# Lightning attention followed by a gated MLP on one core: attention rewritten in units of two heads, with row- and column-tiled matmuls in a fixed order on TensorE

## Chip, cores and metric

The kernel runs on one core of one Trainium2 chip. The metric is device time in microseconds (us) of the whole program. Every time quoted is a median of several executions, with the lowest and highest where they matter. An execution counts as fast or slow: slow is one that lies over 1.5% above the fastest of the same kernel. Medians are of all executions, ratios of fast ones alone.

The engines are TensorE (PE in the profile; PEld is its weight load), VectorE (DVE), ScalarE (ACT), GpSimd (POOL) and SyncE (SP). A line number such as L215 is a line of the kernel that was profiled; experiments that add lines shift the numbers, so each fence is to be read by the names of its tiles.

## The reference

Linear attention with a decay per head, for 4 batches, 8 heads, 768 positions and head size 64, and then an MLP whose gate mixes positions. Cut to what matters:

```python
def _attn_ref(q, k, v, lam):                     # blocks of 64 positions
    for b in range(nb):
        intra = einsum('bhic,bhjc->bhij', qb, kb) * Dmask    # lam ** (i - j) for i >= j
        intra = einsum('bhij,bhjd->bhid', intra, vb)
        inter = einsum('bhid,bhde->bhie', qb * lam_pow, kv_state)
        out[:, :, sl] = intra + inter
        kb_dec = kb * rev_pow                                # lam ** (block - 1 - j)
        kv_state = lam_block * kv_state + einsum('bhsd,bhse->bhde', kb_dec, vb)

def _moe_ref(x, w_in, w_spatial, b_spatial, w_out):          # x: 4 x 768 x 512
    h = maximum(x @ w_in, 0)                                 # 1024 columns
    u, v = h[..., :512], h[..., 512:]
    v_n = (v - mean(v)) / sqrt(var(v) + 1e-6)
    v_s = einsum('ts,bsd->btd', w_spatial, v_n) + b_spatial
    return (u * v_s) @ w_out
```

Both kernels use blocks of 128 positions rather than 64, which is the same function. In both, the 16 units of work are (batch, pair of heads), and the MLP of a batch can start once its four units are done.

## The kernel before

For each unit, stage A loads and transposes q and k; stage B goes through the six blocks one at a time. Per block it issues one score matmul for both heads (q is held as a block-diagonal with zeros in half of it), two matmuls for the state, two for the product with v and two for the old state. One piece of work of the MLP goes between blocks. These are the parts that the change touches:

```python
loglam = const.tile([P, H], FP32)
nc.scalar.activation(out=loglam, in_=lam_bc, func=AF.Ln)
# ... (four more Ln, one per pair of heads, from loads of lam of their own)
nc.scalar.activation(out=ldech, in_=loglam, func=AF.Exp, scale=i127mp[:, 0:1])
# ... (more Exp; ScalarE ends up changing between Ln and Exp)

# stage B of unit u: attention of one pair of heads
def issue_akv(m):
    pam = psum.tile([P, 384], FP32, tag="bank", name=f"pam_{u}_{m}")
    nc.tensor.matmul(out=pam[:, 0:256], lhsT=kT[:, m * P:(m + 1) * P],      # full array
                     rhs=qT_bd[:, :, m * P:(m + 1) * P], start=True, stop=True)
    for hh in range(2):
        nc.tensor.matmul(out=pam[hh * 64:(hh + 1) * 64, 256:320],           # 64 columns
                         lhsT=kdec[:, m, hh, :], rhs=v_sb[:, m, hh, :],
                         start=True, stop=True)

for m in range(NBLK):
    # ... VectorE: mask of the scores (256 elements), new state
    if m + 1 < NBLK:
        issue_akv(m + 1)
    for hh in range(2):
        nc.tensor.matmul(out=pout[orows, ocols], lhsT=v_sb[:, m, hh, :], rhs=a_sb[:, hh, :], ...)
        if m > 0:
            nc.tensor.matmul(out=pout[orows, ocols], lhsT=sold,
                             rhs=qT_bd[:, hh, m * P:(m + 1) * P], ...)
    # ...
    yield

# driver
for u in range(NU):
    gB, gA = ...                                  # stage B of u, stage A of u + 3
    for step, _ in enumerate(gB):
        # ... next(gA)
        if fi < len(fillers):
            fillers[fi](); fi += 1                # transposes of w_spatial
        elif moe_pend:
            moe_pend.pop(0)()                     # one piece of the MLP
```

## Time and profile before

| | before |
|---|---|
| time | 218.57 us, median of 3 (218.17 to 220.46) |
| span of the profiled execution | 221.2 us |
| TensorE busy | 188.9 us (85%) |
| VectorE, ScalarE busy | 128.0, 115.4 us |
| changes of tiling on TensorE | 278 |

A page is read from the top: the busy shares say which engine could be the bound; the 40 slices say when; the chain that ended last says what each part of the time waited for. A busy TensorE need not be streaming columns. For that I take the trace of its instructions and walk from the start of each matmul to the start of the next. From each interval I take the columns at the clock then granted (0.056 us for 128 columns, 0.107 at half clock; these are measured). If two neighbours have different tilings (rows by columns of the array in use), up to 0.13 us of the rest is put down to the change of tiling. What then remains is waiting. Columns that run at half clock are counted at the full rate, with the loss put in a row of its own. This account is used throughout. It adds up to the span. The trace of before lacks 9 of its 1412 matmul records, all of 512 columns, so some 2 us of its columns appear as waits. The columns of one and the same kernel come out 2 to 3 us apart from run to run, so differences below that are not read from it.

### The profile page before, as it was taken

How to read it: one execution, taken by the hardware profiler on the slowest of the kernel's cores; microseconds unless marked ns; L12 is line 12 of the kernel's file. 1: busy time of each engine (PE TensorE's matmuls, PEld its weight loads, DVE VectorE, ACT ScalarE, POOL GpSimd, SP SyncE). 2: the span in 40 equal slices, each digit the busy share in tenths (PEclk: the TensorE clock that was granted, in tenths of full speed). 3: DMA queues.
4: the chain of work that ended last, by engine and by line, in shares of the span. 5: the costliest groups of instructions: out<-in, count | busy, mean ns of one | idle time of the engine just before them, and what ended most of it. 6: DMA issues, size and time to landing. Idle time of an engine off the chain costs nothing.

```text
span 221.2 us, 3795 instructions
## 1 busy us (share of the span) xinstructions
PE 188.9 (85%) x1403; PEld 102.2 (46%) x1412; DVE 128.0 (58%) x355; ACT 115.4 (52%) x217; POOL 83.1 (38%) x110
## 2 busy tenths in 40 slices
PE   0204988899899989999997999999999999998992
PEld 0202644556555556644444455554444565454640
DVE  5106676446879783865789717784698544181420
ACT  7997431666957982116265733023435901679032
POOL 8999144973799771553522200202000000000000
PEclk9999999999999999999999569999999999999998
DMA  4999999993999998959995130506700000700025
GB/s 26 114 130 153 205 186 162 135 126 24 101 108 120 119 66 56 74 70 141 225 66 36 12 27 0 36 3 98 225 3 0 0 3 0 285 0 0 3 90 195
DMA packets 81505, 18.92 MB, mean 86 GB/s; under 512 B 76496, under 2 KB 77904, under 8 KB 81488
## 3 DMA queue, kind: packets, MB, share of 16 engines
q0 software_dynamic: 77248, 12.39, 75.4%
q1 hardware_dynamic: 4240, 6.30, 8.0%
q8 instruction: 11, 0.18, 0.4%
q14 instruction: 6, 0.05, 0.1%
HBM read 24.78 MB, written 6.29 MB: 140 GB/s over the span
## 4 chain that ended last, share of the span: by engine, by line
PE 59%; DMA 14%; POOL 12%; DVE 6%; ACT 4%; issue 3%; ACTq 0%; POOLq 0%
PE pvs L336 14%; PE pu L322 8%; DMA wsp_raw<-in_moe_w_spatial_dram 8%; PE po L354 7%; PE pv L295 7%; PE pam L233 5%; PE pam L236 4%; PE pout L262 4%; POOL q_sb L179 3%; POOL k_sb L181 3%; PE pvs L339 2%; DMA out_dram<-o_sb 2%; DMA k_sb<-in_k_dram 2%; DVE qbd L207 2%; ACT vn_sb L313 2%
## 5 line engine op out<-in xcount | busy, mean ns | idle before, releaser
L250 DVE TENSOR_TENSOR a<-pam,qlkm 128x256 bf16<-128x256 f32 x96 | 39.6, 419 | 15.1 <-PE pam L236 14.5
L185 POOL DMA_DIRECT2D v_sb<-in_v_dram x28 | 23.3, 853 | 51.7 <-PE pout L266 37.9
L233 PE MATMUL pam<-qbd,kT 128*128 128x256 bf16 x96 | 30.8, 321 | 9.7 <-ACT kT L213 9.5
L336 PE MATMUL pvs<-wt_sb,vn_sb 128*128 128x384 bf16 x192 | 37.0, 326 | 1.0 <-ACT vn_sb L313 0.7
L254 DVE SCALAR_TENSOR_TENSOR sst<-sst,l,pam 128x64 bf16<-128x64 bf16 x96 | 26.1, 272 | 14.6 <-PE pout L266 11.7
L358 ACT ACTIVATE o_sb<-po 128x512 f32<-128x512 f32 x24 | 14.3, 597 | 34.2 <-PE po L354 28.8
L342 DVE TENSOR_TENSOR gatedT<-pvs,uT 128x384 bf16<-128x384 f32 x32 | 17.8, 558 | 24.7 <-PE pvs L339 24.6
L262 PE MATMUL pout<-a,v_sb 128*64 128x128 bf16 x192 | 27.1, 256 | 5.1 <-DVE a L250 5.0
L181 POOL DMA_DIRECT2D k_sb<-in_k_dram x28 | 24.6, 887 | 10.4 <-ACT kdec L189 5.2
L322 PE MATMUL pu<-xT,win_sb 128*128 128x384 bf16 x128 | 26.9, 356 | 1.4 <-DVE qbd L207 1.4
L179 POOL DMA_DIRECT2D q_sb<-in_q_dram x28 | 24.4, 879 | 7.1 <-PE pam L236 4.6
L336 PEld LDWEIGHTS <-vn_sb 128*128 128x128 bf16 x192 | 18.3, 98 | 14.0 <-ACT vn_sb L313 1.6
L189 ACT ACTIVATE kdec<-k_sb,ldech 128x384 bf16<-128x384 bf16 x32 | 18.2, 606 | 12.7 <-PE pam L236 10.9
L236 PE MATMUL pam<-v_sb,kdec 128*64 128x64 bf16 x192 | 23.9, 233 | 0.0
L295 PE MATMUL pv<-win_sb,xT 128*128 128x512 bf16 x93 | 23.0, 380 | 0.5 <-DVE qbd L207 0.3
L354 PE MATMUL po<-wout_sb,gatedT 128*128 128x512 bf16 x90 | 22.5, 380 | 0.7 <-DVE qbd L207 0.4
L298 ACT ACTIVATE vh<-pv 128x512 bf16<-128x512 f32 x24 | 14.3, 597 | 13.3 <-PE pv L295 13.0
L299 DVE BATCH_NORM_STATS2 st<-vh 128x6 f32<-128x512 bf16 x24 | 16.6, 690 | 7.6 <-ACT vh L298 7.4
L266 PE MATMUL pout<-qbd,sst 128*64 128x128 bf16 x160 | 20.8, 249 | 0.0
L207 DVE TENSOR_TENSOR qbd<-pqt,lq 64x768 bf16<-64x768 bf16 x32 | 17.7, 553 | 5.4 <-PE pqt L199 4.9
L262 PEld LDWEIGHTS <-v_sb 128*64 128x64 bf16 x192 | 14.7, 121 | 13.1 <-issue 9.8
L236 PEld LDWEIGHTS <-kdec 128*64 128x64 bf16 x192 | 12.2, 116 | 18.2 <-issue 14.5
(63 smaller groups left out, 224.1 us busy)
## 6 DMA issues: line engine op xcount, KB each, us to landing
out_dram<-o_sb SPq DMA_DIRECT2D x24, 256.0 KB, 2.0
q_sb<-in_q_dram POOLq DMA_DIRECT2D x32, 96.0 KB, 3.9
k_sb<-in_k_dram POOLq DMA_DIRECT2D x32, 96.0 KB, 3.8
v_sb<-in_v_dram POOLq DMA_DIRECT2D x32, 96.0 KB, 3.8
wsp_raw<-in_moe_w_spatial_dram POOLq DMA_DIRECT2D x1, 1152.0 KB, 17.2
win_sb<-in_moe_w_in_dram POOLq DMA_DIRECT2D x1, 1024.0 KB, 8.7
wout_sb<-in_moe_w_out_dram POOLq DMA_DIRECT2D x1, 512.0 KB, 10.5
bspbc_sb<-in_moe_b_spatial_dram POOLq DMA_DIRECT2D x1, 192.0 KB, 11.1
```

Source lines behind the costliest of these rows:

```text
L179: nc.gpsimd.dma_start(out=q_sb[:, :, hh, :], in_=q[b, h].rearrange("(m p) d -> p m d", p=P))
L181: nc.gpsimd.dma_start(out=k_sb[:, :, hh, :], in_=k[b, h].rearrange("(m p) d -> p m d", p=P))
L185: nc.gpsimd.dma_start(out=v_sb[:, :, hh, :], in_=v[b, h].rearrange("(m p) d -> p m d", p=P))
L233: nc.tensor.matmul(out=pam[:, 0:256], lhsT=kT[:, m * P:(m + 1) * P], rhs=qT_bd[:, :, m * P:(m + 1) * P], start=True, stop=True)
L236: nc.tensor.matmul(out=pam[hh * 64:(hh + 1) * 64, 256:320], lhsT=kdec[:, m, hh, :], rhs=v_sb[:, m, hh, :], start=True, stop=True)
L250: nc.vector.tensor_tensor(out=a_sb, in0=pam[:, 0:256].rearrange("p (h c) -> p h c", c=P), in1=qlkm_g[g], op=ALU.mult)
L254: nc.vector.scalar_tensor_tensor(out=snew, in0=sold, scalar=lam128_g[g][:, 0:1], in1=pam[:, 256:320], op0=ALU.mult, op1=ALU.add)
L262: nc.tensor.matmul(out=pout[orows, ocols], lhsT=v_sb[:, m, hh, :], rhs=a_sb[:, hh, :], start=True, stop=(m == 0))
L295: nc.tensor.matmul(out=pv, lhsT=xT[gg][:, nt * P:(nt + 1) * P], rhs=win_sb[:, gg, DH:DFF], start=(gg == 0), stop=(gg == NCH - 1))
L322: nc.tensor.matmul(out=pu, lhsT=win_sb[:, gg, ft * P:(ft + 1) * P], rhs=xT[gg][:, b * S + th * THW: b * S + (th + 1) * THW], start=(gg == ...
L336: nc.tensor.matmul(out=pvs, lhsT=vn_sb[:, nt, dc * P:(dc + 1) * P], rhs=wt_sb[:, st, th * THW:(th + 1) * THW], start=(st == 0), stop=False)
L354: nc.tensor.matmul(out=po, lhsT=gatedT[:, ft, nt * P:(nt + 1) * P], rhs=wout_sb[:, ft, :], start=(ft == 0), stop=(ft == NCH - 1))
```

## The change

The intent is to spend less of TensorE's time between matmuls. The work of a unit is put in blocks of equal shape: all transposes, then six scores, ten state matmuls, ten and twelve output matmuls. Scores use two row tiles (64 rows each, one head in each, so that no half is zeros). The decays move into k, into q and into a single mask, which needs fewer operations on VectorE. A whole batch of q, k and v comes in three transfers (the first batch in parts). The order of TensorE's instructions is fixed by hand, with four pieces of the MLP at a time. The core of the diff:

```diff
-            nc.tensor.matmul(out=pam[:, 0:256], lhsT=kT[:, m * P:(m + 1) * P],
-                             rhs=qT_bd[:, :, m * P:(m + 1) * P], start=True, stop=True)
-            for hh in range(2):
-                nc.tensor.matmul(out=pam[hh * 64:(hh + 1) * 64, 256:320],
-                                 lhsT=kdec[:, m, hh, :], rhs=v_sb[:, m, hh, :],
-                                 start=True, stop=True)
+        pam = ps_a.tile([P, 2, 4, P], FP32, tag="pam", name=f"pam_{u}_{i}")
+        for c in range(3):
+            for hh in range(2):
+                t = 3 * i + c
+                nc.tensor.matmul(out=pam[:, hh, c, :],
+                                 lhsT=kT[hh * D:(hh + 1) * D, t * P:(t + 1) * P],
+                                 rhs=qblk(u, hh, t), start=True, stop=True)
 ...
+        for c in range(1, NBLK):                 # outputs from the states: 64 x 64 tiles
+            for hh in range(2):
+                rows = slice(hh * D, (hh + 1) * D)
+                nc.tensor.matmul(out=po[c // 3][rows, c % 3, :], lhsT=s_sb[rows, c - 1, :],
+                                 rhs=qblk(u, hh, c), start=c in (1, 3), stop=False,
+                                 skip_group_check=True)
+        for c in range(NBLK):                    # outputs from the masked scores: 128 x 64
+            for hh in range(2):
+                rows = slice(hh * D, (hh + 1) * D)
+                nc.tensor.matmul(out=po[c // 3][rows, c % 3, :], lhsT=v_in[b][:, 2 * g + hh, c, :],
+                                 rhs=a_sb[:, hh, c, :], start=False, stop=c in (2, 5),
+                                 skip_group_check=True)
 ...
-            nc.scalar.activation(out=vn_sb[:, nt, :], in_=vh_sb[:, st, :],
-                                 func=AF.Identity,
-                                 bias=nbias[:, st:st + 1], scale=rstd[:, st:st + 1])
+                    nc.vector.tensor_scalar(out=vn[:, s, :], in0=vh[:, s, :],
+                                            scalar1=mv[:, s, 0:1], scalar2=rstd[:, s:s + 1],
+                                            op0=ALU.subtract, op1=ALU.mult)
 ...
+    with tc.manual_schedule(engines={PE}):
+        # ... units 0 and 1 are begun
+        for u in range(NU):
+            b, g = divmod(u, NG)
+            if u + 2 < NU:
+                gate = kdec_unit(u + 2)
+                if u + 2 == NG - 1:
+                    load_batch(1, gate)          # k by SyncE after the gate; q, v by GpSimd
+            if g == 2 and b + 2 < B:
+                load_batch(b + 2, gate)
+            if u + 1 < NU:
+                scores_unit(u + 1, 0)
+            out_unit(u)
+            # ... at g == 3 the pieces of batch b join the list
+            fill(4)
+            if u + 1 < NU:
+                scores_unit(u + 1, 1)
+                kv_unit(u + 1)
+            if u + 2 < NU:
+                trans_unit(u + 2)
+            fill(4 if u % 2 else 3)
```

Cuts are marked "...".

## The prediction

> **What bounds the kernel now.** I read the page first (busy shares, the 40 slices, the chain), then the timeline of a dense stretch, of the start and of the cold part, then the groups by form.
>
> ```profile
> PE 188.9 (85%) x1403; PEld 102.2 (46%) x1412; DVE 128.0 (58%) x355; ACT 115.4 (52%) x217; POOL 83.1 (38%) x110
> ...
> PE   0204988899899989999997999999999999998992
> ...
> PEclk9999999999999999999999569999999999999998
> ...
> PE 59%; DMA 14%; POOL 12%; DVE 6%; ACT 4%; issue 3%; ACTq 0%; POOLq 0%
> ```
>
> TensorE (PE) is busy in nearly every slice from 20 us on and is 59% of the chain that ended last; the other 26% of DMA and POOL lie in the first 72 us. So there are two parts: a start that waits, then a PE that sets the pace. But busy is not streaming. The timeline of a warm, dense stretch:
>
> ```profile
> 86.25 1.14 PE L336 MATMUL pvs<-wt_sb,vn_sb 128*128 128x384 bf16 x6
> ...
> 87.39 0.50 PE L199 MATMUL pqt<-ident,q_sb 128*128 128x128 bf16 x6
> 87.73 0.27 PE L233 MATMUL pam<-qbd,kT 128*128 128x256 bf16 x1
> 87.93 0.22 PE L236 MATMUL pam<-v_sb,kdec 128*64 128x64 bf16 x2
> 87.98 0.23 PE L262 MATMUL pout<-a,v_sb 128*64 128x128 bf16 x2
> 88.04 0.22 PE L266 MATMUL pout<-qbd,sst 128*64 128x128 bf16 x2
> ...
> 88.60 0.27 PE L233 MATMUL pam<-qbd,kT 128*128 128x256 bf16 x1
> 88.81 0.22 PE L236 MATMUL pam<-v_sb,kdec 128*64 128x64 bf16 x2
> 88.96 0.28 PE L233 MATMUL pam<-qbd,kT 128*128 128x256 bf16 x1
> ```
>
> Six 384-column matmuls span 1.14 us and one lasts 0.326 (group mean), so (1.14-0.326)/5 = 0.162 us each; six 128-column transposes give (0.50-0.219)/5 = 0.056. Two 64-row-output matmuls of a pair start together (x2 in 0.22), so a pair costs one: 87.98 to 88.04 is 0.056 for a 128-column pair, 87.93 to 87.98 is 0.05 for a 64-column pair. But from a full-array matmul to a column-tiled pair it takes 88.60 to 88.81 = 0.21 us, where 256 columns stream in 0.107; and back 88.81 to 88.96 = 0.15 for 64 columns. Each change of tiling costs about 0.1 us. Walking the whole PE trace with these stream times I get 278 changes at 0.11 us = 31 us, and 28 us of gaps beyond streaming and changes, 10 of them before 20 us. The rest, some 158 us, is streaming (136 us if all of it were warm, below) and the end.
>
> The start:
>
> ```profile
> 8.16 0.69 PE L199 MATMUL pqt<-ident,q_sb 128*128 128x128 bf16 x5 [8.16 <-DMA q_sb<-in_q_dram]
> ...
> 19.61 0.40 PE L233 MATMUL pam<-qbd,kT 128*128 128x256 bf16 x1 [9.52 <-ACT kT L213]
> ...
> 26.02 0.85 PE L199 MATMUL pqt<-ident,q_sb 128*128 128x128 bf16 x6
> ```
>
> Scores begin only at 19.6 us, because ScalarE first does nine table loads of 1.28 us (rows of that name in the groups by form), most of them swaps between Ln and Exp, and then the decay tables. And six transposes take 0.85 us at 26 us against 0.50 at 87: PE runs at half rate (0.107 us per 128 columns) until about 56 us, and again from 121 to 131, where PEclk shows 5 and 6. The chain names what feeds the middle of the start:
>
> ```profile
> 18.65 17.17 DMA wsp_raw<-in_moe_w_spatial_dram
> 35.86 0.49 issue
> 36.35 5.13 DMA k_sb<-in_k_dram
> ```
>
> The weights (2.9 MB as bf16, 5.8 MB read as f32) take until about 36 us, some 330 GB/s of reads; the attention inputs behind them wait.
>
> **What the Trainium skill says.** "TensorEngine Tiling (Array Packing)", Key Properties: changing the tiling mode, not just the tile, drains the engine. The trace agrees: about 0.1 us each. The same page, Gotcha 1 (PSUM Pressure): different row tiles cannot access one PSUM bank at once. No row tile is in this trace; it bears on a rival below. "TensorE: Matmul & The Clock Gate", Part 1: the clock is half when idle and full after sustained activity; the 0.107 against 0.056 agrees. "VectorE: DVE Perf Modes", the perf-mode tier table: a tensor_scalar on bf16 in SBUF can run at four elements a cycle; no row of before is of that sort at size, so I use it only for an estimate.
>
> **The change part by part.** MLP matmuls are the same in number and shape: 224 of 384 columns (pvs with bias) and 128 (pu) at 0.162, 192 of 512 at 0.216 (pv, po) = 36.3+20.7+41.5 = 98.5 us of streaming.
>
> Attention, streaming when warm. Before: 192 transposes x 0.056 = 10.8, 96 scores of 256 columns (half of them zeros) x 0.107 = 10.3, 96 kv pairs x 0.05 = 4.8, 96+80 output pairs x 0.056 = 9.9; 36 wsp transposes 2.0; 37.8 in all. After: transposes of 64 columns in 192 pairs, 10.8; scores 96 row-tiled pairs of 128 columns, 5.4 if the pair runs together; kv 80 pairs, 4.0; outputs 80+96 pairs, 9.9; wsp 2.0; 32.1 in all. So streaming falls only from 136 to 131 us.
>
> Tiling changes: in the instruction order of PE I count 278 before and 104 after (scores, kv, transposes and outputs come in blocks per unit, MLP pieces four at a time). At 0.1 us: 31 to about 10.5 us, a gain of 20 us. This is the largest term.
>
> ScalarE: 7 of the 9 opening table loads go (one for Ln and one for Exp stay), so scores can begin near 11 us rather than 19.6. vn moves to VectorE (17.3 us off; 24 operations there at an estimated 0.25 us = 6), the transposed k is always copied on ScalarE (16 x 0.81 = 12.9 against 6.5), as is every xT (32 x 0.49 = 15.6 against 7.7), wt 6 x 0.81. Sum some 102 us against 115.
>
> VectorE: mask 32 x (0.42-0.267+0.8) = 0.95 for 768 elements (the 256-element row is 0.419, about 0.267 of it elements) = 30.5 against 39.6; states 16 x 0.22 + 64 x 0.272 = 21 against 26; q 16 x 0.56 = 9 against 17.7; no xT or kT copies (13 off); bn and gate unchanged at 38.7; vn 6; setup 3. About 108 against 128. Neither engine becomes the bound: per unit with its MLP pieces PE needs about 9.4 us, VectorE 6.6, ScalarE 5.8.
>
> Loads: q packs two rows (3,072 packets a batch, not 6,144), k goes as f32 by the SP queue. A batch is 4.7 MB read, in three transfers, and unit 4's transposes need the whole q of batch 1, which stands behind the weights. Fixed PE order puts those transposes before the output of unit 3 and so before any MLP of batch 0. Landing estimate: batch 0 4.7 + weights 5.8 + k and q of batch 1 3.1 = 13.6 MB at 330 GB/s = 41 us, plus 2 of latency: 43 to 45 us. Before that, units 0 to 3 have no filler; start 11.5, about 3 of prologue and three rounds of some 5.2 us (mask, mask, states, q on VectorE 3.8, plus waits) end near 30. So PE idles from about 30 to 44.
>
> Path: 44 us; then the PE work left: 131 - 8 (attention of the first units) = 123 streaming, 82 changes x 0.105 = 8.6; a cold first window 2; waits for PSUM in the MLP pieces. For these, before in its warm middle (60 to 180 us) has 9.6 us in 120, 8%; two banks with pu at 0.65 of PE against 0.48 plus latency on ScalarE stay tight; 8% of 131 = 10. End after the last matmul: evacuation 0.6, output transfer 2.0, closing, 4 in all as before. 44+123+8.6+2+10+4 = 191.6. The tail's vn wait of before (about 4 us at 199 to 204) is gone, since pieces of u lie in between. I take 189.
>
> **Rivals.** (1) The pairs do not run together, for the output pairs from the states put two row tiles in one bank: +4.5 us (80 x 0.056), and for scores +5.4: about 199. For: the skill's gotcha. Against: the two halves write different partitions, and scores use two banks. (2) The transfers are faster or in another order and q of batch 1 lands by 36: about 181. For: slice 5 moved 205 GB/s of bf16, over 330 read. Against: 128-byte packets in before never passed 135. (3) ScalarE or VectorE in their given order hold PE in each unit, as two banks and strict order leave no slack: 20 us of waits rather than 10, 200. For: the margin of 0.65 over 0.48 plus latency. Against: in the list of waits of before it is those engines that wait for PE (o_sb 28.8 us, gatedT 24.6), and PE's own waits on them in the MLP are under 2 us each. (4) Another half-clock spell like that of 121 to 131: +5. (5) The waits are nearly gone because the pieces are spread by hand: 181.
>
> **Range and chances.** Rivals move it by 8 to 10 us either way and can add: 189, 8 in 10 from 175 to 203. To be within 2% (214 to 223) at least three of the adverse ones must come together. Faster 0.96, same 0.03, slower 0.01.
>
> **What would show it.** Right: a PE gap near 30 to 44 us ended by the q load of batch 1; changes of tiling near 104 with about 0.1 us each; pairs of scores within 10 ns of each other; PE in 95% of the slices after 45; VectorE near 108 and ScalarE near 102 busy. Wrong: pairs 0.05 us apart (rival 1); no gap at 30 (rival 2); waits of PE on ScalarE or VectorE above 15 us after 45 (rival 3); PEclk below 9 late (rival 4). If changes between row and column tiles cost 0.2 rather than 0.1, +8.

## The result, and the profile after

| | before | after |
|---|---|---|
| time | 218.37 us, median of 4 (217.67 to 220.46) | 198.5 us, median of 4 (198.18 to 198.84) |
| span of the profiled execution | 221.2 us | 196.7 us |
| ratio | | 0.9065, 95% interval 0.9004 to 0.9127 |

A ratio here is the mean time of one kernel's fast runs over the mean of the other's fast runs of the same rounds, so it is not quite the ratio of the medians.

The page of the changed kernel, from busy shares to the shares of the chain:

```profile
PE 153.4 (78%) x1668; PEld 89.3 (45%) x1668; DVE 104.5 (53%) x252; ACT 99.3 (50%) x181; POOL 23.2 (12%) x28
...
PE   0341766103779599999999699999999999999992
...
PEclk9999985555589999999999999999999999999998
DMA  5999999999999939931697000043000004400025
...
PE 59%; DMA 26%; ACT 4%; DVE 4%; POOL 4%; issue 1%; POOLq 0%; ACTq 0%
```

Against the rows of before: TensorE is now nearly idle in slices 8 and 9 and most of 10 (the gap lasts from 35 to 47 us), the DMA share of the chain has risen from 14% to 26%, and the row of the clock shows half from 28 to 56 us. From 59 us on TensorE is busy in nine tenths of each slice or more, but for two slices at 64 and 108 us and the last.

The timeline of TensorE around the gap (start, length, engine, line, tiles, count, and in brackets the idle time before and what ended it):

```profile
34.61 0.48 PE L228 MATMUL pkv<-v_in,kdec 128*64 128x64 bf16 x10
47.21 0.85 PE L187 MATMUL pq<-ident,q_in 128*64 128x128 bf16 x12 [12.12 <-DMA q_in<-in_q_dram]
...
52.44 5.24 PE L285 MATMUL pv<-win_sb,xT 128*128 128x512 bf16 x16
...
59.20 0.35 PE L228 MATMUL pkv<-v_in,kdec 128*64 128x64 bf16 x10 [1.24 <-DMA v_in<-in_v_dram]
```

The transposes of unit 4, the first of batch 1, wait 12.1 us for the whole q of their batch. The first piece of the MLP stands behind them and starts at 52.4 us. The length of 0.85 us for twelve transposes (they run in pairs) shows the half clock.

The timeline of TensorE in a warm stretch, in which a unit's scores and outputs stand between pieces of the MLP:

```profile
101.30 0.34 PE L215 MATMUL pam<-qT,kT 64*128 64x128 bf16 x6
101.57 0.47 PE L247 MATMUL pat<-qT,s 64*64 64x128 bf16 x10
101.97 0.53 PE L253 MATMUL pat<-a,v_in 128*64 128x128 bf16 x12
102.42 1.90 PE L285 MATMUL pv<-win_sb,xT 128*128 128x512 bf16 x8
```

28 attention matmuls take 102.42 - 101.30 = 1.12 us. Six scores in three pairs are 3 x 0.056 = 0.17 of the 0.27 us to the next group, ten state outputs in five pairs 0.28 of 0.40, twelve score outputs in six pairs 0.34 of 0.45. What is left over is 0.10, 0.12 and 0.11 us: one change of tiling each.

The waits of TensorE (us in total, times, longest):

```profile
PE pq L187 <- DMA q_in<-in_q_dram: 21.3, 3, 12.1
PE pam L215 <- ACT kT L198: 8.7, 4, 4.9
...
PE pwt L333 <- ACT wt_sb L335: 2.3, 2, 2.1
PE pkv L228 <- DMA v_in<-in_v_dram: 1.2, 1, 1.2
```

The larger ones lie before 60 us, but for the 2.1 us of the w_spatial transposes (pwt), which wait for their own copies at 65 us. And the groups by line, for the two operations whose cost came out above the estimate:

```profile
L257 ACT ACTIVATE xT<-pat 128x384 bf16<-128x384 f32 x32 | 16.7, 593 | 24.8 <-PE pat L253 24.8
...
L294 DVE TENSOR_SCALAR vn<-vh,mv,rstd 128x512 bf16<-128x512 bf16 x24 | 8.1, 408 | 0.1
```

The account of TensorE's time, by the walk described above:

| us | before | after | difference |
|---|---|---|---|
| until the first matmul | 8.2 | 8.3 | +0.1 |
| columns, at the full rate | 130.9 | 127.0 | -3.9 |
| lost to the half clock | 16.0 | 8.3 | -7.7 |
| changes of tiling (278, 104) | 30.9 | 10.7 | -20.2 |
| waits | 27.7 | 35.8 | +8.1 |
| gaps of at most 0.01 us between matmuls | 2.9 | 2.5 | -0.4 |
| after the start of the last matmul | 4.6 | 4.0 | -0.6 |
| span | 221.2 | 196.7 | -24.5 |

The largest term is the changes of tiling; the new wait for q of batch 1 eats a part of it. One caution belongs to this table: the profiled execution of before is a long one. In all runs the time is some 2 us above the span, so 221.2 us of span is a time of about 223 us (an estimate), where the median is 218.4. The medians differ by 19.9 us and not by 24.5, so about 4.6 us of the last column belong to that execution and not to the change. It ran at half clock from 121 to 131 us, which cost about 4 us in the walk. No trace of a faster execution of before was kept, so how much of the -7.7 us in the row of the half clock comes from the change is not shown. The number of changes of tiling is the same in every execution. The experiments ask three things: is a change of tiling really the cause of the 20 us, what sets the start, and what can be had from it.

### The profile page after: what moved, and what is told of

It reads as the page before. It is cut to its first block, busy times and chain, and to the rows that moved or that the text cites. A ratio compares the mean times of both kernels' runs of the same rounds, so it can differ in the third digit from the quotient of the medians.

```text
span 196.7 us, 3964 instructions
## 1 busy us (share of the span) xinstructions
PE 153.4 (78%) x1668; PEld 89.3 (45%) x1668; DVE 104.5 (53%) x252; ACT 99.3 (50%) x181; POOL 23.2 (12%) x28
## 4 chain that ended last, share of the span: by engine, by line
PE 59%; DMA 26%; ACT 4%; DVE 4%; POOL 4%; issue 1%; POOLq 0%; ACTq 0%
DMA v_in<-in_v_dram 26%; PE pvs L310 16%; PE po L318 10%; PE pu L302 10%; PE pv L285 9%; PE pam L215 3%; PE pvs L312 3%; PE pat L253 3%; PE pat L247 2%; POOL q_in L69 2%; ACT wt_sb L335 2%; PE pkv L228 1%; DVE a L218 1%; PE pq L187 1%; PE pk L191 1%; POOL v_in L74 1%
## 5 line engine op out<-in xcount | busy, mean ns | idle before, releaser
L218 DVE TENSOR_TENSOR a<-pam,amask 128x768 bf16<-128x768 f32 x32 | 30.4, 950 | 27.0 <-PE pam L215 27.0
L310 PE MATMUL pvs<-wt_sb,vn 128*128 128x384 bf16 x192 | 36.5, 326 | 0.0
L313 DVE TENSOR_TENSOR gT<-pvs,uT 128x384 bf16<-128x384 f32 x32 | 17.8, 557 | 23.0 <-PE pvs L312 22.9
L174 ACT ACTIVATE kdec<-k_in,ldec 128x384 bf16<-128x384 f32 x32 | 17.8, 606 | 22.9 <-DMA k_in<-in_k_dram 15.8
L257 ACT ACTIVATE xT<-pat 128x384 bf16<-128x384 f32 x32 | 16.7, 593 | 24.8 <-PE pat L253 24.8
L187 PE MATMUL pq<-ident,q_in 128*64 128x128 bf16 x192 | 9.8, 249 | 21.3 <-DMA q_in<-in_q_dram 21.3
L321 ACT ACTIVATE o<-po 128x512 f32<-128x512 f32 x24 | 14.3, 597 | 21.1 <-PE po L318 15.5
L310 PEld LDWEIGHTS <-vn 128*128 128x128 bf16 x192 | 18.3, 98 | 12.2
L288 DVE BATCH_NORM_STATS2 st<-vh 128x6 f32<-128x512 bf16 x24 | 16.4, 685 | 12.1 <-ACT vh L287 12.1
L318 PE MATMUL po<-wout_sb,gT 128*128 128x512 bf16 x96 | 22.4, 379 | 0.1
L215 PE MATMUL pam<-qT,kT 64*128 64x128 bf16 x192 | 12.1, 239 | 10.1 <-ACT kT L198 8.7
L233 DVE SCALAR_TENSOR_TENSOR s<-s,l,pkv 128x64 bf16<-128x64 bf16 x64 | 17.7, 276 | 1.2
L304 ACT ACTIVATE uT<-pu 128x384 bf16<-128x384 f32 x32 | 15.5, 491 | 4.2 <-PE pu L302 4.1
L215 PEld LDWEIGHTS <-kT 64*128 64x128 bf16 x192 | 6.0, 100 | 19.6 <-ACT kT L198 10.8
```

The lines of the kernel that those rows point to most:

```text
L174: i = nc.scalar.activation(out=kd[:, hh], in_=k_in[b][:, h], func=AF.Copy, scale=ldec[:, h:h + 1])
L187: nc.tensor.transpose(out=pq[hh * D:(hh + 1) * D, r, m * P:(m + 1) * P], in_=q_in[b][:, 2 * g + hh, r, m, :], identity=ident)
L215: nc.tensor.matmul(out=pam[:, hh, c, :], lhsT=kT[hh * D:(hh + 1) * D, t * P:(t + 1) * P], rhs=qblk(u, hh, t), start=True, stop=True)
L218: nc.vector.tensor_tensor(out=st[u]["a"][:, :, 3 * i:3 * i + 3, :], in0=pam[:, :, 0:3, :], in1=amask[:, 2 * g:2 * g + 2].unsqueeze(2).broa ...
L233: nc.vector.scalar_tensor_tensor(out=s_sb[:, m], in0=s_sb[:, m - 1], scalar=l128[:, g:g + 1], in1=pkv[:, m], op0=ALU.mult, op1=ALU.add)
L257: nc.scalar.activation(out=xT[b][:, g, i * HW_:(i + 1) * HW_].rearrange("p (c d m) -> p c m d", c=3, m=2), in_=po[i].rearrange("p c (m d) ...
```

## The experiments

Twelve kernels ran, and all gave a correct result. They ran in four sets, each with its own runs of the kernel before on the same chip (medians 219.03, 218.47, 219.38 and 219.02 us). Diffs are against the changed kernel unless another is named.

### 1. The output pairs interleaved again

Only the order of one group of matmuls changes: for each block the pair from the state and the pair from the scores follow each other, as in the kernel before. Number, shape and data of all matmuls stay; the changes of tiling go from 104 to 232.

```diff
-        for c in range(1, NBLK):
-            ...  # all pairs from the states
-        for c in range(NBLK):
-            ...  # all pairs from the scores
+        for c in range(1, NBLK):
+            s_pair(c)
+            if c == 1:
+                a_pair(0)
+            a_pair(c)
```

> The changed kernel with the output matmuls of a unit in another order: state pair and mask pair of each block in turn, rather than all state pairs and then all mask pairs. Same matmuls, same operands; 8 more changes of tiling in each of 16 units, 104 to 232 in all. Theory (each change of tiling costs 0.095 us, and that is where 20 us of the gain lie): the 96 more in the 12 units after the start's wait add 9.1 us, those of the first four units are mostly hidden in the wait: 207.5, 206 to 211. Rival (the grouping helps through fewer waits between engines, not through the array): under 3 us more, 198 to 201.

Measured: 207.43 us (207.19 to 208.92), ratio 0.946, 0.9389 to 0.9531. The timeline of TensorE in the same stretch of work, where the 22 output matmuls of a unit now stand in ten groups instead of two:

```profile
103.65 0.24 PE L247 MATMUL pat<-qT,s 64*64 64x128 bf16 x2
103.83 0.30 PE L254 MATMUL pat<-a,v_in 128*64 128x128 bf16 x4
104.06 0.24 PE L247 MATMUL pat<-qT,s 64*64 64x128 bf16 x2
```

From one group of two to the next it is 0.17 to 0.18 us where a pair streams in 0.056: each change costs 0.114 to 0.117 us. The walk gives 26.6 us for 232 changes against 10.7 for 104, so +15.9 us. The waits are 7.5 us shorter (28.3 against 35.8; 3.3 of it in the waits for q, 18.0 against 21.3, since the slower attention fills time that was waited anyway), and the half clock costs 1.3 us more. (Most of the rest are waits for the states on VectorE, 3.8 us in the changed kernel and not in the list here.) The sum of these, 9.7 us, is about the +9 us of the time. The theory holds: the changes are a cost of their own, and grouping is what removes it. It is not that two matmuls in a row write the same place in PSUM: in the kernel before the two output pairs do that without a change of tiling, and follow each other after 0.056 us (87.98 and 88.04 in the prediction's timeline). But what the changes add to TensorE's account and what they add to the time differ: 128 changes are 15.9 us of the one and 9 us of the other, as part of them falls into time that was waited anyway. The other parts of the change, such as the mask, the decays in k and q, and vn on VectorE, were not undone one by one.

### 2. The three scores of one head after the other

This asks whether two row tiles must be neighbours in program order to run side by side.

```diff
-        for c in range(3):
-            for hh in range(2):
+        for hh in range(2):
+            for c in range(3):
```

> The changed kernel with the six score matmuls of a block row ordered by head (three of head 0, then three of head 1), so that two neighbours use the same row tile. Theory (row-tiled pairs run side by side, 3 ns apart, and save half): of 96 pairs, 72 after the start's wait lose 0.053 us less one pair each 3 that still meets: 3 to 4 us more, 201 to 203. Rival (the pair's saving is not on the path): within 1 us, 198 to 199.5.

Measured: median 198.69 us; three fast runs of 198.23 to 198.69, two slow ones of about 202; ratio of the fast runs 0.9042, 0.8947 to 0.9136. So nothing changed, and the expectation missed. The profiled run was a slow one, so of its trace I use only the spacing inside one group. The six scores of a unit start at 124.719, .729, .785, .795, .841 and .851 us: still three slots of 0.056, with 0.010 us within a couple where the changed kernel has 0.003 to 0.004. "TensorE: Matmul & The Clock Gate", Part 3 of the Trainium skill, says that matmuls start strictly in program order; with the order as written, two neighbours on one row tile would then need a slot each. The program built again from this run's kernel does have that order: three on the rows of head 0, then three on those of head 1. The trace does not show which row tile a matmul used, so whether TensorE took them in another order, or the two tiles overlap in some other way, stays open. What the run does show is that the order of heads inside this group costs nothing.

### 3. Batch 2 loaded later

In the changed kernel q and v of batch 1 share the DMA engines with k of batch 2, issued at 41.4 us, with first packets at 46. Here the loads of a later batch are issued two units later.

```diff
-            if g == 2 and b + 2 < B:
-                load_batch(b + 2, gate)
+            if g == 0 and 1 <= b and b + 1 < B:
+                load_batch(b + 1, gate)
```

> The changed kernel with the loads of batch 2 (k first) asked for two units later, so that they no longer share the DMA engines with v of batch 1. v of batch 1 should land some 7 us earlier than 59.2. Theory (the wait that counts is for q of batch 1, which lands at 47.2 and ends a PE gap of 12.1 us; the wait for v is 1.2 us): 197.3, 1 to 1.5 us less. Rival (the chain of waits is right that v of batch 1, 26% of the span, sets the restart): 191 to 193.

Measured: 205.68 us (204.39 to 208.3), ratio 0.9356, 0.9294 to 0.9418. This missed both expectations, and the edit failed in its aim: ScalarE ran ahead, so that k of batch 2 was still issued at 43.9 us, with first packets at 48, and v of batch 1 landed at 58.8 us rather than 59.2. The loads of batch 3 now met the output transfers. The timeline at that place:

```profile
101.69 0.60 ACT L321 ACTIVATE o<-po 128x512 f32<-128x512 f32 x1 [2.61 <-DMA out_dram<-o]
...
102.33 5.89 PE L285 MATMUL pv<-win_sb,xT 128*128 128x512 bf16 x15 [4.50 <-ACT o L321]
```

A copy of the output waited for a free staging buffer, that is for an output transfer, and TensorE waited 4.5 us for the copy. The clock was at half from 100.6 to 107.4 us, which begins within this wait. The lesson is one for the next experiments: where a batch's loads stand matters to the outputs as well as to the inputs.

### 4. Batch 1 in parts

The wait of 12.1 us is for a transfer of eight heads of which unit 4 needs two. Here q and v of batch 1 come in four parts, two heads each, between the weights; k in four parts as well. This version also had the later loads of experiment 3.

```diff
+    alloc_in(1)
+    def load_part(g):
+        load_q(1, 2 * g, 2 * g + 2)
+        load_v(1, 2 * g, 2 * g + 2)
     load_win(DH, DFF)
+    load_part(0)
     load_win(0, DH)
+    load_part(1)
     ...  # w_spatial, b_spatial
+    load_part(2)
+    load_part(3)
     ...  # w_out
-                if u + 2 == NG - 1:
-                    load_batch(1, gate)
+                if u + 2 < NG:
+                    for gk in {2: (0,), 3: (1, 2, 3)}[u + 2]:
+                        li = load_k(1, 2 * gk, 2 * gk + 2)
+                        ...  # released by the kdec of unit u + 2, as before
```

> The changed kernel with the loads of batch 1 in four parts by unit, as batch 0 has them, set between the weights (the part for unit 4 right after the first half of w_in), and batch 2 as in the run before. No matmul changes. Theory (the start waits for q of batch 1 behind the weights): the gap of 12.1 us before the transposes of unit 4 falls to 2 or less, and the clock is up earlier: 186 to 189. Rival (the DMA engines are the bound for the first 60 us: the same 15.2 MB must land in any order, and the wait reappears at the weights or at later units): 194 to 198.

Measured: 196.02 us (195.27 to 197.03), ratio 0.8929, 0.8861 to 0.8997. Its timeline of TensorE, the first MLP of batch 0 and a later place:

```profile
41.85 5.31 PE L295 MATMUL pv<-win_sb,xT 128*128 128x512 bf16 x16
...
91.62 6.12 PE L295 MATMUL pv<-win_sb,xT 128*128 128x512 bf16 x16 [4.88 <-ACT o L331]
```

The gap is gone: the MLP starts 10.6 us sooner than the 52.44 of the changed kernel. But the collision of experiment 3 is here too (4.9 us, and half clock from 89.9 to 96.7). So against the changed kernel this run measured two things at once. Against the run of experiment 3 it differs in the split alone, and is 9.7 us faster (196.02 against 205.68), which is the clean measure of it.

The next run takes the second away: batch 2 is loaded at unit 4 and batch 3 at unit 6.

```diff
-            if g == 0 and 1 <= b and b + 1 < B:
-                load_batch(b + 1, gate)
+            if u == 4:
+                load_batch(2, gate)
+            if u == 6:
+                load_batch(3, gate)
```

> The run with split loads of batch 1 again, with the loads of batch 3 asked for at unit 6 as in the changed kernel, so that they no longer meet the output transfers at 85 to 105 us, where that run lost 5.0 us of PE waiting for o_sb and then 2.6 us of half clock. Theory (those 7.6 us were of my own edit, and the wait for q of batch 1 is worth some 9 us): 187 to 190. Rival (the DMA engines are behind anyway, and the loss moves elsewhere): 194 to 197.

Measured: 188.58 us (187.27 to 190.42), ratio of the three fast runs 0.8621, 0.859 to 0.8653. The theory holds: about 10 us lie in the load of batch 1, and this version beats both kernels. The edit both splits the load and sets its parts ahead of some of the weights; no run moved the whole load ahead unsplit, so which of the two counts is open. Its profiled run was the slowest of the four (190.42 us), so I read from its trace where waits stand, not their sum. TensorE's timeline in its first part:

```profile
20.07 0.50 PE L225 MATMUL pam<-qT,kT 64*128 64x128 bf16 x6 [4.74 <-ACT kT L208]
...
28.62 0.50 PE L225 MATMUL pam<-qT,kT 64*128 64x128 bf16 x6 [3.59 <-ACT kT L208]
...
42.17 0.31 PE L257 MATMUL pat<-qT,s 64*64 64x128 bf16 x2 [0.68 <-DVE s L243]
43.20 0.61 PE L295 MATMUL pv<-win_sb,xT 128*128 128x512 bf16 x1
```

Now units 1 and 2 wait 4.7 and 3.6 us for a copy of kT. ScalarE had put a kdec of a later unit ahead of that copy, and that kdec waited for its k. Experiments 6 and 7 take this up.

### 5. The table loads, in the kernel before

The prediction gave the opening of the kernel before to nine table loads on ScalarE. This run removes six of them there, and leaves the rest of that kernel as it is.

```diff
-    lamhd_g = []
-    for g in range(NG):
-        ...  # two loads of lam per pair of heads
     for g in range(NG):
-        nc.scalar.activation(out=logl_g[g], in_=lamhd_g[g], func=AF.Ln)
+        for hh in range(2):
+            rows = slice(hh * 64, (hh + 1) * 64)
+            nc.vector.tensor_copy(out=logl_g[g][rows, :],
+                                  in_=loglam[rows, 2 * g + hh:2 * g + hh + 1])
```

> The kernel before with one part of the change alone: the logarithms of the decays are copied from one Ln, so that 2 of 8 table loads of the Ln-Exp swapping stay in the opening (and 8 small loads go). Scores should begin near 11 us rather than 19.6. Theory (the opening is not on the path: the chain runs through the issue of loads on GpSimd and the weights, which end at 36 us and do not move): 216 to 219.5, at most 1% less. Rival (the opening of ScalarE is on the path): 8 us less, 210 to 212.

Measured: median 219.7 us (216.35 to 221.07), ratio of the two fast runs 0.9968, 0.9909 to 1.0027: no gain that the runs show, and the rival's 210 to 212 is ruled out. TensorE's timeline of this version at its first score:

```profile
11.63 0.40 PE L228 MATMUL pam<-qbd,kT 128*128 128x256 bf16 x1 [2.61 <-ACT kT L208]
```

and its chain of waits (start, length, what):

```profile
18.60 17.64 DMA wsp_raw<-in_moe_w_spatial_dram
...
36.77 3.93 DMA k_sb<-in_k_dram
```

(The profiled run was one of the slow two; I read only the times of events from it.) Scores begin at 11.6 rather than 19.6 us, and nothing follows from it, for the chain goes through the weights and then k as before: w_spatial has landed at 36.2 us, against 35.8. The waits only move: the walk finds 10.2 us before 20 us and 3.7 from 20 to 40 in the kernel before, and here 3.7 before 20 and 11.4 from 20 to 40. Eight microseconds on an engine that waits for a transfer later are worth none.

### 6. ScalarE in the written order

Fixing ScalarE's order as well as TensorE's takes the kdec out of the way of the kT copies. First on the changed kernel, for the whole run:

```diff
-    with tc.manual_schedule(engines={PE}):
+    with tc.manual_schedule(engines={PE, mybir.EngineType.Activation}):
```

> The changed kernel with ScalarE held to program order as PE is, so that the copies of the transposed k no longer stand behind a k scaling that waits for a load (4.9 us at 15 to 20). No transfer is asked for in another order. Theory (PE waits for q of batch 1 till 47.2 whatever it did before): 197.5 to 199.5, the gap before unit 4 longer by some 5 us. Rival (the wait of ScalarE in the opening is on the path): 193 to 194.

Measured: 204.59 us (204.04 to 206.17), ratio 0.9386, 0.934 to 0.9432. TensorE's timeline at the gap:

```profile
47.23 0.85 PE L187 MATMUL pq<-ident,q_in 128*64 128x128 bf16 x12 [16.73 <-DMA q_in<-in_q_dram]
```

The part of the expectation on the opening holds: the first units end 4.6 us sooner (the gap is 16.7 rather than 12.1 us), and q lands at 47.23 against 47.21 as if nothing had happened. What was not expected is the +6 us: the waits are 43.7 us in all against 35.8, and since q lands at the same time, the loss lies after the gap. The largest single piece is 2.7 us of waiting for a copy of u on ScalarE between 140 and 160 us (3.2 us of waits there, 0.5 in the changed kernel); the rest is spread. The trace fits a ScalarE whose written order is worse later; no run tested that by itself.

Second, on the version of experiment 4 (188.6 us), for the first three rounds only:

```diff
     with tc.manual_schedule(engines={PE, mybir.EngineType.Activation}):
         ...  # units 0 and 1 are begun
+        rounds(range(3))
+    with tc.manual_schedule(engines={PE}):
+        rounds(range(3, NU))
```

> The version with split loads and batches 2 and 3 loaded later (188.6 us), with ScalarE kept in the written order for the first three rounds only, so that a copy of kT no longer stands behind a kdec that waits for its k transfer; the later rounds are ordered as before. Theory (the early units are held by that order on ScalarE, some 10 us of PE waits before 30 us, and now that batch 1 comes in parts, finishing early is worth something): the waits of 3.6 and 4.7 us of the scores for kT are gone, the MLP of batch 0 starts 3 to 6 us earlier, 183 to 186 us. Rival (the k and q transfers of batch 1 and the weights of the MLP set the start of the MLP anyway): the waits move to those transfers, 187.5 to 190.

Measured: 192.61 us (192.07 to 192.88), ratio 0.881, 0.8754 to 0.8865, so 3 to 4 us slower than the 188.6, outside both expectations. TensorE's timeline:

```profile
37.08 0.85 PE L201 MATMUL pk<-ident,kdec 128*64 128x128 bf16 x12 [4.49 <-ACT xT L267]
...
43.96 0.50 PE L225 MATMUL pam<-qT,kT 64*128 64x128 bf16 x6 [6.03 <-ACT kT L208]
```

The early waits of 4.7 and 3.6 us are down to 1.1 and 0.9 (at 16.5 and 22.3 us), and two new ones of 4.5 and 6.0 us stand at 37 and 44. In both, ScalarE itself stood in a kdec, of unit 5 and of unit 6, that waited for its part of k of batch 1; the xT of unit 2 and the kT of unit 4 stood behind it. The loads of k are released by earlier kdec operations, and the written order had moved these: three of the four parts set out between 23.3 and 28.0 us rather than between 19.3 and 25.2.

Third, therefore, the same with all four parts of k released by the kdec of unit 2:

```diff
-            if u + 2 < NG:
-                for gk in {2: (0,), 3: (1, 2, 3)}[u + 2]:
+            if u == 0:
+                for gk in range(NG):
```

> The version with ScalarE in written order for three rounds (192.6 us), with all four parts of k of batch 1 released by the kdec of unit 2 rather than the last three by that of unit 3. Theory (the written order was itself of use, the early waits for kT went, and it lost only because the releases of k of batch 1 hang on ScalarE and so came some 4 us later, which brought new waits of 4.5 and 6.0 us for kdec at 37 and 44 us): the last part of k lands 3 to 6 us sooner, these waits shrink by 4 to 8 us, 184 to 188 us. Rival (the start is bound by the sum of the transfers, so one transfer sooner makes q of batch 1 or the weights later): the waits move to q and to the MLP weights, 190 to 193 us.

Measured: 189.5 us (188.56 to 190.69), ratio 0.8647, 0.8588 to 0.8706. This lies between what theory and rival expected. TensorE's timeline:

```profile
34.33 0.85 PE L201 MATMUL pk<-ident,kdec 128*64 128x128 bf16 x12 [2.74 <-ACT xT L267]
40.44 0.50 PE L225 MATMUL pam<-qT,kT 64*128 64x128 bf16 x6 [5.26 <-ACT kT L208]
42.18 0.32 PE L257 MATMUL pat<-qT,s 64*64 64x128 bf16 x2 [0.68 <-DVE s L243]
```

and the transfer in its chain of waits:

```profile
20.75 17.72 DMA k_in<-in_k_dram
```

The part of k for unit 6 ends its transfer at 37.0 us rather than 39.9, and the scores behind its kdec come at 40.4 rather than 44.0, so the release was the cause of the loss in the run before. But the two waits shrink only from 10.5 to 8.0 us, and the outputs of unit 3, after which the MLP starts, come at 42.18 us. In the version of experiment 4, with ScalarE left alone and its early waits of 8 us, they come at 42.17, and there that part of k ends at 36.2 us. Still, the same 42.2 us does not come from the same cause. Here the chain waits for k until 38.5 us (20.75 + 17.72), and the kdec of unit 6 and the scores follow. In the version of experiment 4 the last transfer in the chain is k of unit 4, which ends at 26.65 us; from there to 42.17 the chain holds masks, states, matmuls at half clock and copies alone, and its kdec of unit 6 starts at 38.27 us after TensorE's pkv, two us after its k. So in this last version the time gained before 30 us turns into waits for k, as the rival has it, with ScalarE's order putting the kdec of unit 6 ahead of the kT of unit 4. That the sum of the transfers sets the first 42 us in general is not shown. A version with that kdec and that kT exchanged was not run.

### 7. The transposes of w_spatial later

On the version of experiment 4, these six groups move behind the pieces of u, for they wait about 2 us for their own copies at 57 us.

```diff
-                    pend[6:6] = w
+                    pend[14:14] = w
```

> The same version (188.6 us) with the six groups of w_spatial transposes put after the eight pieces of u rather than before them. Theory (these transposes wait for each other's copies on ScalarE, some 2 us at about 57 us, for their results share two PSUM banks with the pieces of v): 186.5 to 188. Rival (the copies only move, and hold the pieces of the gate instead): 188 to 190.

Measured: 190.04 us (189.53 to 190.68), ratio 0.8697, 0.8641 to 0.8753. The rival's 188 to 190 is nearer: the copies only moved. The waits for them fell from 2.1 to 1.1 us, and new ones of 0.8 us on the gate's product and 1.1 us on u came up.

Both edits, this and the three rounds of ScalarE order, together:

> Both of these edits together. If each gives what its theory says, they add: 181.5 to 185. If transfers bind the start, as in the rival of the first, 186 to 189.

Measured: 192.39 us (190.12 to 193.66), ratio 0.8745, 0.866 to 0.883. Neither edit gained by itself and they gain nothing together. The version of experiment 4 (ratio 0.8621) stays the best of all, with the one of k released sooner (0.8647) level with it within the intervals.

### 8. TensorE kept busy through the gap

On the changed kernel, 41 matmuls of 512 columns that nobody reads: 32 ahead of the transposes of unit 4, five after them, four ahead of the output of unit 3. They ask whether the half clock after the gap is a cost of the gap.

```diff
+    def keep_warm(n, name):
+        ps = ps_g.tile([P, DM], FP32, tag="pg", name=name)
+        for _ in range(n):
+            nc.tensor.matmul(out=ps, lhsT=ident, rhs=win_sb[:, 0, DH:DFF], start=True, stop=True)
```

> The changed kernel with 41 matmuls of 512 columns into an unused bank in the gap before the transposes of unit 4 and in two short waits after it; nothing reads them. Theory (3.1 us of the time after 47.2 is streaming at half clock, since PE idled for 12 us): the half clock of 47 to 56 goes and 2 to 3.5 us with it: 195 to 196.5. Rival (the clock does not follow these matmuls, or they delay unit 4): 198 to 201.

Measured: 199.75 us (197.89 to 200.88), ratio 0.9142, 0.9101 to 0.9183. The page's row of the clock:

```profile
PEclk9999999997599889999999999999999999999999
```

The clock did rise within the gap, at 37 us. But the spare matmuls ended at 43.2 us, q landed at 49.5 us in this run, and the clock was down again from 47.2 to 54.0 us and from 67.7 to 71.1. The loss to the half clock came to 10.0 us against 8.3. The run gives no answer: the matmuls were too few for this landing, and more of them would have stood in the way of an earlier one. What 8 us at half clock cost, and whether they can be had, is open.

### All runs

The sets ran on different chips, so the order of versions within 2 us of each other is not to be leaned on.

| version | median us | ratio to before |
|---|---|---|
| the change | 198.5 | 0.9065 |
| output pairs interleaved | 207.43 | 0.946 |
| scores of one head after the other | 198.69 | 0.9042 |
| batch 2 later | 205.68 | 0.9356 |
| batch 1 in parts, with the collision | 196.02 | 0.8929 |
| batch 1 in parts | 188.58 | 0.8621 |
| ... with three rounds of ScalarE order | 192.61 | 0.881 |
| ... and k of batch 1 sooner | 189.5 | 0.8647 |
| ... with w_spatial later | 190.04 | 0.8697 |
| ... with both edits | 192.39 | 0.8745 |
| ScalarE in written order throughout | 204.59 | 0.9386 |
| spare matmuls in the gap | 199.75 | 0.9142 |
| before, six table loads less | 219.7 | 0.9968 |

## Why the prediction was right, and where its sum was off

The range held (175 to 203), the direction was right, and the mechanism was the one named: TensorE at the pace, changes of tiling as the largest gain, and a gap ended by q of batch 1. The point estimate was 9.5 us too low. The sum of its path, term by term, with the walk of the changed kernel from 47.2 us on:

| term | predicted us | measured us |
|---|---|---|
| q of batch 1 is there | 44 | 47.2 |
| columns from there on | 123 | 120.8, and 2.3 in gaps of up to 0.01 |
| changes of tiling | 8.6 | 8.6 |
| half clock after the gap | 2 | 3.1 |
| waits after the gap | 10 | 10.6 |
| end | 4 | 4.0 |
| sum | 191.6 | 196.6 |

- **The landing of q of batch 1** is the term that was mis-sized most, by 3.2 us, and in it the bytes and not the rate. I took 13.6 MB at 330 GB/s, the rate from the best stretch of before. The packets that the trace has by 47.2 us make 14.7 MB of reads (those written as bf16 counted double), 326 GB/s in 45 us. So the rate held, and what I left out is about 1 MB: v of batch 1 and k of batch 2 moved before the last of q. The runs of experiments 3 and 6 say the same, 14.4 MB at 328 GB/s (q at 46.0 us) and 14.9 at 330 (47.2). The place of the gap's start was off as well, 35 rather than 30 us, for TensorE's scores waited 8.7 us for kT copies that stood behind a kdec on ScalarE. I had counted such waits as part of the rounds. It did not matter to the time, as the landing ends the gap whenever it starts; the written order on ScalarE shows this, with a start 4.6 us sooner and the same end.
- **The step from 191.6 to 189** had no number behind it but the wait for vn in the tail of before, which the sum did not contain in the first place. It was a credit for a cost that the sum did not hold, 2.6 us of the 9.5.
- **The last 1.8 us** are between the span of the profiled run, 196.7 us, and the median time, 198.5. The sum was worked out in spans and then given as a time. In before the profile fell on a long execution (a span of 221.2 us against a median time of 218.6), which hid this difference.
- **Columns**: 120.8 where 123 was predicted. About 1 us of it (an estimate) is the 60 pairs of 64 columns that make the states after the gap: the prediction took 0.05 us each, and most of them follow each other after 0.031. One sum of the prediction is off too: 221 less 31 less 28 leaves 162 us for streaming and the end and not 158; nothing rests on it.
- **Changes of tiling**: 104 at 0.103 us, 10.7 us, where 10.5 was predicted; before 278 at 0.111. The experiment with interleaved pairs shows that it is a cost of its own and not a label for something else.
- **Rival 1, pairs that do not run together**, is false. Score pairs start 3 to 4 ns apart, and the pairs from the states, two row tiles in one PSUM bank, mostly follow each other after 0.056 us, so they do too. Gotcha 1 of the tiling page, which had spoken for this rival, did not bind here.
- **Rival 2, transfers sooner**, is false in the changed kernel; the experiment with batch 1 in parts is what it would have been worth, 10 us.
- **Rival 3, ScalarE or VectorE holding TensorE**, does not hold after 60 us: 7.3 us of waits in 137 us. Before 60 us it shows, but in the shadow of the transfers.
- **Rival 4, another half-clock spell late**, did not come in the changed kernel. It came in several experiments, twice beginning during a wait of TensorE of over 4 us (batch 2 later, and batch 1 in parts with the collision).
- **The opening**: the prediction put the later start of before down to table loads and named their removal as a part of the change. The table loads were real, but removing them from before gave nothing. In the changed kernel scores start at 11.7 us, and there too the next bound is the load of batch 1: the 4.6 us that the written order on ScalarE gained before the gap brought nothing. I had not given it a number in the sum, so it cost no accuracy, but a reader of the prediction could take it as a gain.
- **A sign that did not come as written**: TensorE in 95% of the slices after 45 us. From 49 us on 25 of 30 slices show a 9; the cold slices after the gap and the two dips are the rest.
- **Busy time**: VectorE 104.5 against some 108 predicted, ScalarE 99.3 against some 102. Inside these, vn took 408 ns each rather than the estimated 250, and xT 593 rather than 490 (it writes with a stride now; whether that is the reason was not tested). The mask took 950 ns, as estimated. The groups of VectorE add up to some 112 us where 104.5 are busy, so neighbours overlap in the records, and a sum of groups, as I took it, comes out high. Neither engine set the pace, so the errors had no effect.

## What to carry to other kernels

Count the changes of tiling in TensorE's instruction order before counting flops: here 174 fewer of them took 20 us off TensorE's account, putting 128 back cost 9 us of time, and no busy share shows them. When an order is fixed by hand, ask which whole transfer its first dependent instruction needs: splitting one load into the parts that units need, and setting the first ones ahead of the weights, gave another 5% on top. Gains on an engine that next waits for a transfer are worth nothing until the transfer moves, and moved loads must be checked against the outputs that they will now meet.

## What the Trainium skill lacked or had wrong

- "TensorEngine Tiling (Array Packing)", Key Properties, says that a change of the tiling mode drains TensorE, but gives no duration. Here it is 0.09 to 0.10 us at full clock in the changed kernel, for each of the six kinds of change, 0.10 to 0.11 into and out of column tiling in the kernel before, and 0.114 to 0.117 between 64x64 and 128x64 when interleaved.
- The same page, Gotcha 1, says that different row tiles cannot access one PSUM bank at the same time. The pairs from the states write two row tiles into different partitions of one bank, and mostly take 0.056 us a pair at full clock, as much as one matmul of 128 columns.
- "TensorE: Matmul & The Clock Gate", Part 3, says that matmuls start strictly in program order. Six scores in the order of one head and then the other still took three slots of 0.056 us, and the time was unchanged (ratio 0.9042 against 0.9065). The program built from the kernel has that order, but the trace does not tell which tile each matmul used, so this is a doubt and not a refutation.
- The same page, Part 1, says that about 3.4 us of sustained activity gives the full clock. In the kernel before TensorE was busy in 80 to 90% of each slice from 20 us on, and its matmuls still ran at 0.107 us per 128 columns until about 56 us; in the walk it streams columns for 24 of the 40 us from 20 to 60, the rest being changes of tiling and short waits. No run here separates busy from streaming, or transposes from other matmuls.
- No page has this of the profile as read here: the row of the granted clock shows 9 until the first record of the clock falls in the trace, even where twelve paired transposes take 0.85 us, the half-clock length (the version with batch 1 in parts, with a mean clock of 0.99 and 11 us lost to the half clock). The length of a known group is the safer reading, and mean clocks of two runs were not comparable here.
- "VectorE: DVE Perf Modes", the perf-mode tier table, puts a tensor_scalar on bf16 in SBUF at four elements a cycle. Its row is for 2048 elements. The 512-element vn with two per-partition scalars took 408 ns, where I had estimated 250 from it; no run here separates a fixed part from the rate, so this corrects my estimate and not the page.
